# Attention and mixture of experts on one core: stores without order among themselves, gates fetched together, deeper buffers

## The chip, the core and the metric

One core of a Trainium2 chip. Its engines run in parallel, each through its own queue in order: TensorE (PE, with its weight loads, PEld), VectorE (DVE), ScalarE (ACT), GpSimd (POOL) and SyncE (SP, which here only issues DMAs). Indirect DMAs (gathers and scatters by a list of indices) are issued on POOL; the weights come through SP's queue. All transfers run on 16 DMA engines. The metric is the device time of one execution in microseconds, median of several runs.

## The reference

Attention over 8 batches, 12 heads, 448 positions and a head size of 64, with capped scores, and behind it a mixture of experts with 3584 tokens of width 768, 8 experts of width 1024, and room for 80 tokens an expert.

```python
scores = cap * np.tanh(scale * np.matmul(q, k.transpose(0, 1, 3, 2)) / cap)
attn = np.exp(scores - max); attn = attn / (sum(attn) + 1e-09)
x = np.matmul(attn, v)                       # to (B * S, H * D)
logits = x @ w_gate; expert_idx = argmax(logits); gate_w = softmax(logits)[expert_idx]
for e in range(E):
    tok_idx = tokens of e, at most `capacity` of them by gate_w
    out[tok_idx] = gate_w[tok_idx, None] * (np.maximum(x[tok_idx] @ w1[e], 0) @ w2[e])
```

Rows of tokens that no expert keeps are zero.

## The kernel before

Attention runs in 24 units (a batch and four heads), software-pipelined, with an order written out by hand; the work between (gates of a batch, ranks of its tokens, lists of kept tokens) is put into gaps by a planner with costs and due times (`background`, with the queues `urgent`, `low` and `bg`). Attention's rows go to DRAM (`xs`), the gate of each token to DRAM (`gd`). The expert stage is built for at most six experts that hold tokens (`NV`): the first four (`NPRE`, experts 0 to 3 below) are known after five of the eight batches, their rows are fetched during attention's end (`first_rows`: three indirect gathers an expert, 128 descriptors each, and DVE transposes). The last two (experts 4 and 5 below) are known only when all tokens are ranked.

An expert is two runs of jobs: "a" is x times w1 in 6 chunks of 512 KB, "b" is h times w2 in 8 chunks of 384 KB; a chunk is 24 matmul records in the trace (L842). The jobs' order on TensorE is a0 a1 b0 a2 b1 a3 b2 b3 a4 a5 b4 b5. Weights come chunk by chunk through SP into a ring of WPRE + WMORE = 8 + 6 buffers; a chunk's DMA waits until the chunk 14 before it is used up.

Behind "b" stands `put`: it scales the rows by the gate (L890 on DVE; for the last expert L885 on ACT and L887 on DVE, in three parts) into the tile ys, of which there is one buffer, and issues three indirect stores on POOL (L892). The framework orders two stores to `out` as it would any two writes to one tensor: the later one waits on POOL until the earlier one has landed. The gates of expert v are fetched on POOL by three indirect DMAs (`gates`, L777) that are issued when "b" of v begins, so behind the stores of the expert before.

Among expert 2's and 3's products the planner lays the last steps of the ranking: flags `gb` on DVE (L491) and tiny matmuls `pd` (L507) that count them; the rank (L1285, L1289); the marks `rh`, half on DVE and half on POOL (L730) with `rt` on POOL (L735); the matmuls `pcp` that place the tokens (L745, L748); the indices (`listed`, L751 to L763); the fetch of the rows of experts 4 and 5 (L784, three buffers xg); their transposes (L1504). TensorE stands at pcp until both halves of `rh` are there, and its queue is in order. On POOL the order is: stores of expert 2, gates of expert 3, `rh`, `rt`, row fetches of experts 4 and 5, stores of expert 3, gates of expert 4, and so on.

Of the kernel before, what the change touches and what calls it, by code (L numbers as in the profile page):

```python
# [16 lines left out]
B, H, S, D = 8, 12, 448, 64  # L17
# [27 lines left out]
KD = DM // 128  # L45
KF = F // 128
WPRE = 8
WMORE = 6
DIRECT = (20, 23)
NG = SL // 32  # L50
QF = F // 4
# [63 lines left out]
def attn_moe(ctx, tc, q2, k, v, cap, wg, w1, w2, capacity, ct, out):  # L115
# [65 lines left out]
    sg0 = consts.tile([128, NPRE, NG], I32, name="sg0")  # L181
# [389 lines left out]
    def prune(krow, sm, pl):  # L571
# [83 lines left out]
            gather_rows(z["ga"], tks, gi0, OB * S)  # L655

        def rows_out():
            scatter_rows(gp_tile, tks, z["ga"], si0, sg0)

        def gp_tile(key):  # L660
            return tile_([32, NPRE, NG], F32, key)
# [9 lines left out]
        def first_rows():  # L671
            for v in range(NPRE):
                for i in range(3):
                    yield 300, lambda v=v, i=i: fetch(v, i), int(v == i == 0)
                for i in range(3):
                    yield 400, lambda v=v, i=i: lay(v, i), 3 * int(i == 0)
        yield 300, heads, 0
        yield 200, use(0, counts), 1
        steps = order(sm)
# [75 lines left out]
    def scatter_rows(tile_of, tk, a, si, sg):  # L755

        o = tile_of("to")
        nc.vector.tensor_scalar(o, tk, 0.0, BIG, op0=ALU.is_equal, op1=ALU.mult)
        nc.vector.tensor_tensor(o, o, tk, op=ALU.add)
        for i in range(4):  # L760
            w = slice(32 * i, 32 * i + 32)
            nc.vector.tensor_scalar(si[w], o, float(i - 4), None, op0=ALU.add)
            nc.vector.tensor_scalar(sg[w], a, 0.25, -1.0, op0=ALU.mult, op1=ALU.add)  # L763

    def indices(sm, tk, n):
# [4 lines left out]
        scatter_rows(lambda key: sm.tile([32, n, NG], F32, name=key, tag=key), tk, a, si, sg)  # L770
        return gi, si, sg

    def gates(fp, sg, tag, n=T):
# [6 lines left out]

    def fetched(fp, gi, tag, n=T, to=None):

        xg = to if to is not None else fp.tile([128, NP * 32], F32, name=f"xg{tag}", tag="xg", bufs=3)
        nc.gpsimd.indirect_dma_start(out=xg, out_offset=None, in_=xs[0:n].rearrange("t i p c -> (t i) (p c)"),  # L784
                                     in_offset=bass.IndirectOffsetOnAxis(ap=gi, axis=0))
        return xg
# [90 lines left out]
        product(yp, h, ws[KD:], DM)  # L877
        put(fp, yp, gt, si, tag)

    def put(fp, yp, gt, si, tag, last=False):  # L880
        ys = fp.tile([128, NG, QD], F32, name=f"ys{tag}", tag="ys", bufs=1)
        if last:
            for g in range(NG):
                if g % 2 == 0:
                    nc.scalar.activation(ys[:, g], spot(yp, g, QD), AF.Copy, scale=gt[:, g:g + 1])  # L885
                else:
                    nc.vector.tensor_scalar(ys[:, g], spot(yp, g, QD), gt[:, g:g + 1], None, op0=ALU.mult)  # L887
        else:
            y = yp.rearrange("p a (b c) -> p (a b) c", c=QF)[:, 0:NG, 0:QD]
            nc.vector.tensor_tensor(ys, y, gt.rearrange("p (g a) -> p g a", a=1).broadcast_to([128, NG, QD]), op=ALU.mult)  # L890
        for g in range(NG):
            nc.gpsimd.indirect_dma_start(out=out.rearrange("t (i c) -> (t i) c", c=QD), out_offset=bass.IndirectOffsetOnAxis(ap=si[:, g:g + 1], axis=0),  # L892
                                         in_=ys[:, g], in_offset=None, bounds_check=4 * T - 1, oob_is_err=False)

    def compare(sm, tk):

# [594 lines left out]

    def listed():
        tk = fin["tk"] = fin["pcp"][0:32, 0:3 * NV].rearrange("p (e k) -> p e k", k=3)
        fin["gi"], fin["si"], fin["sg"] = indices(fr, tk, NV)
# [24 lines left out]
    st["vector"] = vector  # L1519
    hp, hs, ht, yp, gt = {}, {0: hs0}, {}, {}, {}  # L1520
    more(WPRE + WMORE)
    for i, (k_, vi, kk) in list(enumerate(jobs))[KD:]:
        more(i + WPRE + WMORE)
        if i + 3 == len(jobs):
            while bg or low:
                background(1e9)
            decide(fin["m"], compare(fr, fin["early"]))
        if k_ == "a" and kk == 0:
            st["there"](vi)
        if k_ == "a":  # L1530
            if kk == 0:
                if vi < NV - 1:
                    hp[vi] = pfh.tile([128, 2, 512], F32, name=f"hp{vi}", tag="hp")
                else:
                    hp[vi] = tuple(misc(f"hp{vi}{i_}") for i_ in "ab")
            chunk(hp[vi], xv[vi] if vi >= NPRE else xt0[vi], wts[i], kk, KD - 1, F)
            if kk == KD - 1:
                hs[vi] = relu(fp, hp[vi], f"v{vi}", 1 + (vi == NV - 1))
        else:
            if kk == 0:  # L1540
                yp[vi] = (pft.tile([128, 2, 512], F32, name=f"yp{vi}", tag="ht") if vi < NV - 1 else
                          (pft.tile([128, 512], F32, name=f"yp{vi}a", tag="ht"), pfh.tile([128, 512], F32, name=f"yp{vi}b", tag="hp")))
                gt[vi] = gates(fp, sg0[:, vi], f"v{vi}", OB * S) if vi < NPRE else gates(fp, fin["sg"][:, vi], f"v{vi}")
            chunk(yp[vi], ht[vi], wts[i], kk, KF - 1, DM)
            if kk == KF - 1:
                put(fp, yp[vi], gt[vi], (si0 if vi < NPRE else fin["si"])[:, vi], f"v{vi}", vi == NV - 1)
# [57 lines left out]
```

## Time and profile before

| | us |
|---|---|
| median of 3 runs | 521.21 (519.57 to 523.6) |
| the profiled execution | 522.82 |
| its span, first to last instruction | 521.0 |

| engine | busy us | share of the span |
|---|---|---|
| PE | 467.9 | 90% |
| PEld | 252.3 | 48% |
| DVE | 247.9 | 48% |
| ACT | 324.6 | 62% |
| POOL | 244.4 | 47% |

The mean granted TensorE clock is 0.958 of full speed. A row of the timelines reads: start, duration, engine, line, operation, output and input tiles, count, and in brackets the engine's idle time just before and what ended it. The time of an indirect DMA on POOL is that of its issue; it lands later. Where a wait was for several things, the view names the one that came last by its own reckoning.

### The profile page before, as it was taken

The page shows a single profiled execution, that of the slowest core. Times are in us where ns is not written, and L with a number is a line of the kernel's source. Part 1 is how long each engine was busy: PE and PEld are TensorE (multiplying, and loading weights), DVE is VectorE, ACT ScalarE, POOL GpSimd, SP SyncE. Part 2 cuts the span into 40 slices and gives each one's busy share as a digit, 9 for nine tenths or more (in the row PEclk, how much of TensorE's full clock was granted, in tenths as well). Part 3 has the DMA queues.
Part 4 walks back from the last instruction along what each step waited for, and adds up shares of the span by engine and source line. Part 5 has one row for each costly group of instructions (what it writes and reads, how often), then busy time and mean ns, then how long its engine had stood idle before and what let it go on. Part 6 is the DMA issues. An engine that isn't in the chain of part 4 may idle for free. (4 is left out here: it accounts for less than half of the span.)

```text
span 521.0 us, 21478 instructions
## 1 busy us (share of the span) xinstructions
PE 467.9 (90%) x9591; PEld 252.3 (48%) x9591; DVE 247.9 (48%) x761; ACT 324.6 (62%) x311; POOL 244.4 (47%) x160
## 2 busy tenths in 40 slices
PE   7899999999999999999999999999999976189930
PEld 3344444544444545444554455354576654146820
DVE  1033643564365555667785837655378360040000
ACT  5999899899899989989998979730111100001100
POOL 1766566665655666556566046623101422453051
PEclk9999999999999999999999999999799989589985
DMA  6866786585685696474456738485679979267400
GB/s 165 232 180 179 196 245 180 161 229 171 188 255 153 181 260 180 119 216 127 120 156 165 213 103 253 140 299 172 195 263 352 383 235 348 111 185 256 157 29 16
DMA packets 68647, 101.12 MB, mean 194 GB/s; under 512 B 12833, under 2 KB 50993, under 8 KB 68545
## 3 DMA queue, kind: packets, MB, share of 16 engines
q1 hardware_dynamic: 66048, 96.23, 61.6%
q0 software_dynamic: 2304, 3.26, 2.2%
q8 instruction: 77, 1.26, 1.0%
q14 instruction: 26, 0.20, 0.1%
q10 hardware_dynamic: 192, 0.17, 0.1%
HBM read 76.12 MB, written 23.80 MB: 192 GB/s over the span
## 5 line engine op out<-in xcount | busy, mean ns | idle before, releaser
L1152 ACT ACTIVATE e<-sc,scl 128x896 f32<-128x896 f32 x168 | 163.7, 1006 | 27.5 <-PE sc L1151 19.9
L1156 ACT ACTIVATE e<-e,capt 128x1792 f32<-128x1792 f32 x96 | 153.4, 1598 | 0.0
L1162 POOL TENSOR_TENSOR t<-e 128x896 f32<-128x896 f32 x44 | 92.8, 2110 | 101.7 <-ACT e L1156 100.6
L1151 PE MATMUL sc<-qt,kt 64*32 64x448 f32 x2304 | 132.7, 547 | 4.4 <-ACT e L1152 3.9
L1171 PE MATMUL av<-e,vr 128*32 128x224 f32 x2304 | 129.1, 355 | 1.0 <-DMA vr<-in_v_dram 0.5
L1164 POOL TENSOR_TENSOR t<-t,e 128x896 f32<-128x896 f32 x44 | 92.7, 2107 | 39.5 <-PE sc L1151 19.1
L1171 PEld LDWEIGHTS av<-e,vr 128*32 128x32 f32 x2304 | 67.8, 109 | 61.1 <-issue 18.0
L1211 DVE STREAM_TRANSPOSE st<-sp 128x448 f32<-128x448 f32 x24 | 15.6, 650 | 119.7 <-PE sp L1201 115.8
L892 POOL DMA_INDIRECT out_dram<-ysv,si x18 | 21.0, 1168 | 92.3 <-DMA out_dram<-ysv,si 41.2
L1151 PEld LDWEIGHTS sc<-qt,kt 64*32 64x32 f32 x2304 | 33.0, 106 | 57.6 <-issue 42.7
L842 PE MATMUL hp<-w,xt 128*32 128x256 f32 x720 | 48.6, 393 | 4.2 <-issue 2.6
L842 PE MATMUL yp<-w,thv 128*32 128x192 f32 x960 | 48.0, 350 | 1.3 <-issue 1.3
L1203 PE MATMUL av<-e,vr 64*32 64x224 f32 x384 | 42.9, 350 | 0.2 <-issue 0.2
L1203 PE MATMUL av<-e,vx 64*32 64x224 f32 x384 | 41.3, 350 | 0.0
L842 PEld LDWEIGHTS yp<-w,thv 128*32 128x32 f32 x960 | 34.4, 117 | 12.1 <-issue 4.4
L842 PEld LDWEIGHTS hp<-w,xt 128*32 128x32 f32 x720 | 25.7, 112 | 23.2 <-issue 10.6
L1203 PEld LDWEIGHTS av<-e,vr 64*32 64x32 f32 x384 | 20.1, 106 | 22.5 <-issue 13.1
L418 DVE TENSOR_SCALAR_CACHE_REDUCE gb<-krow,kc 112x896 bf16<-112x896 f32 (+7 forms) x36 | 30.1, 884 | 0.0
L1201 PE MATMUL sp<-e,ones 64*32 64x224 f32 x384 | 28.7, 350 | 0.4 <-issue 0.4
L1224 DVE TENSOR_TENSOR x<-av,r 128x448 f32<-128x448 f32 x48 | 27.8, 620 | 2.4
L1233 DVE STREAM_TRANSPOSE xb<-x 128x448 f32<-128x448 f32 x48 | 28.1, 624 | 0.8
L858 ACT ACTIVATE hsv<-hp 128x768 f32<-128x768 f32 x5 | 4.1, 811 | 33.5 <-PE hp L842 25.5
(241 smaller groups left out, 444.0 us busy)
## 6 DMA issues: line engine op xcount, KB each, us to landing
w<-in_w_dram SPq DMA_DIRECT2D x36, 512.0 KB
w<-in_w_dram SPq DMA_DIRECT2D x48, 384.0 KB
vr<-in_v_dram SPq DMA_DIRECT2D x24, 512.0 KB
out_dram<-zero SPq DMA_DIRECT2D x14, 768.0 KB
xs<-xb SPq DMA_DIRECT2D x32, 336.0 KB
kt<-in_k_dram SPq DMA_DIRECT2D x46, 224.0 KB
qt<-in_q_dram SPq DMA_DIRECT2D x46, 224.0 KB
vx<-in_v_dram SPq DMA_DIRECT2D x48, 32.0 KB
```

Source lines behind the costliest of these rows:

```text
L418: nc.vector.tensor_scalar(g, krow[:, x:y], kp, 0.0, op0=ALU.is_ge, op1=ALU.add, accum_out=a)
L842: nc.tensor.matmul(spot(ps, g, q)[32 * j:32 * j + 32], of(g), w[:, q * j:q * j + q], start=(kk == 0 and g % 2 == 0), stop=(kk == last and ...
L1151: nc.tensor.matmul(ps[32 * m:32 * m + 32, h, :S], st["k", u][w, pr, y:y + 32], st["q", u][w, pr], start=True, stop=True)
L1152: nc.scalar.activation(st["e", u][:, 2 * x:2 * x + 2], ps[:, :, :S], AF.Tanh, scale=scl)
L1156: nc.scalar.activation(e, e, AF.Exp, scale=capt)
L1162: nc.gpsimd.tensor_tensor(t1, e[:, 0:2], e[:, 2:4], op=ALU.add)
L1164: nc.gpsimd.tensor_tensor(st["es", u, pr], st["es", u, pr], e[:, 4:6], op=ALU.add)
L1171: nc.tensor.matmul(st["av", u, i][32 * g:32 * g + 32, HQ * f:HQ * f + HQ], st["v", u][:, g // 2, g % 2, c, 32 * f:32 * f + 32], chunk_of(u ...
L1201: nc.tensor.matmul(st["sp", u][32 * g:32 * g + 32, HQ * i:HQ * i + HQ], st["ones"][w, 0:32], e, start=(part == 0), stop=(part == 1))
L1203: nc.tensor.matmul(st["av", u, i][32 * g:32 * g + 32, HQ * f:HQ * f + HQ], last_of(u, pr, h, i)[w, 32 * f:32 * f + 32], e, start=False, st ...
L1224: nc.vector.tensor_tensor(st["x", u][:, :, w], st["av", u, i][:, :S].rearrange("p (f s) -> p f s", f=2), st["r", u][:, w].rearrange("p (a ...
L1233: nc.vector.transpose(st["xt", b][:, :, j, :], st["x", u][:, f].rearrange("p (a b) -> p a b", b=32))
```

## The change

- The stores of result rows are declared independent of one another (`others`): a store then waits for its scaled rows, and for no other store.
- The gates of experts 0 to 3 are fetched by three indirect DMAs with 128 indices each (32 an expert) into one tile gq, as the last items of `first_rows`; those of experts 4 and 5 in the same manner into gq2, behind their row fetches. When "b" of an expert begins, four ACT copies lay its gates out over the 128 partitions (`gates_of`). The index steps change with that (`gate_rows`).
- Two buffers for ys (from one), six for fetched rows xg (from three), ten more weight buffers behind the first eight (from six).

```diff
-WMORE = 6
+WMORE = 10
...
+            for i in range(NG):
+                yield 100, lambda i=i: gates_at(gq, sg0, i, NPRE, OB * S), 0
...
+    def gate_rows(a, sg, n):
+        for e in range(n):
+            nc.vector.tensor_scalar(sg[32 * e:32 * e + 32], a[:, e], 0.25, -1.0, op0=ALU.mult, op1=ALU.add)
+
+    def gates_at(to, sg, g, n, m):
+        nc.gpsimd.indirect_dma_start(out=to[0:32 * n, g:g + 1], out_offset=None, in_=gd[0:m],
+                                     in_offset=bass.IndirectOffsetOnAxis(ap=sg[0:32 * n, g:g + 1], axis=0))
+
+    def gates_of(fp, packed, e, tag):
+
+        gt = fp.tile([128, NG], F32, name=f"gt{tag}", tag="gt")
+        for i in range(4):
+            nc.scalar.copy(gt[32 * i:32 * i + 32], packed[32 * e:32 * e + 32])
+        return gt
...
-        xg = to if to is not None else fp.tile([128, NP * 32], F32, name=f"xg{tag}", tag="xg", bufs=3)
+        xg = to if to is not None else fp.tile([128, NP * 32], F32, name=f"xg{tag}", tag="xg", bufs=2 * NG)
...
-        ys = fp.tile([128, NG, QD], F32, name=f"ys{tag}", tag="ys", bufs=1)
+    def put(fp, yp, gt, si, tag, last=False, others=None):
+        ys = fp.tile([128, NG, QD], F32, name=f"ys{tag}", tag="ys", bufs=2)
...
+            if others is not None:
+                for o in others:
+                    tc.declare_no_dep(w.ins, o.ins, reason="rows of different tokens")
+                others.append(w)
...
+        for i in range(NG):
+            low.append((100, lambda i=i: gates_at(gq2, fin["sg"][:, 0], i, NV - NPRE, T), 0))
...
-                gt[vi] = gates(fp, sg0[:, vi], f"v{vi}", OB * S) if vi < NPRE else gates(fp, fin["sg"][:, vi], f"v{vi}")
+                gt[vi] = gates_of(fp, gq, vi, f"v{vi}") if vi < NPRE else gates_of(fp, gq2, vi - NPRE, f"v{vi}")
```

## Rows read from the trace of the kernel before

**Rows 1.** The page: GB/s in 40 slices of 13.0 us; the chain's last piece.

```profile
GB/s 165 232 180 179 196 245 180 161 229 171 188 255 153 181 260 180 119 216 127 120 156 165 213 103 253 140 299 172 195 263 352 383 235 348 111 185 256 157 29 16
...
510.96 0.69 POOL out_dram L892
```

**Rows 2.** Waits from 380 us: who waited for whom, us in total, times, longest.

```profile
POOL out_dram L892 <- DMA out_dram<-ysv,si: 41.2, 11, 5.8
...
PE pcp L745 <- POOL rh L730: 13.7, 1, 13.7
```

**Rows 3.** Timeline of POOL from 395 us: gates, stores, marks, row fetches.

```profile
408.74 0.94 POOL L777 DMA_INDIRECT gtv<-gd,sg  x1 [0.30 <-issue]
415.32 2.48 POOL L892 DMA_INDIRECT out_dram<-ysv,si  x1 [5.64 <-DVE ysv L890]
...
428.37 1.15 POOL L892 DMA_INDIRECT out_dram<-ysv,si  x1 [4.66 <-DMA out_dram<-ysv,si]
...
432.39 0.94 POOL L777 DMA_INDIRECT gtv<-gd,sg  x1 [0.31 <-issue]
439.79 1.02 POOL L892 DMA_INDIRECT out_dram<-ysv,si  x1 [6.45 <-DVE ysv L890]
...
453.39 0.69 POOL L730 TENSOR_TENSOR rh<-oh,bo 112x288 bf16<-112x288 bf16 x1
...
456.23 0.98 POOL L784 DMA_INDIRECT xgv<-xs,gi  x1 [1.93 <-DVE to L758]
...
464.86 0.94 POOL L784 DMA_INDIRECT xgv<-xs,gi  x1 [0.30 <-issue]
```

**Rows 4.** Timeline of DVE from 380 us: scalings, indices, the last transpose.

```profile
414.29 0.76 DVE L890 TENSOR_TENSOR ysv<-yp,gtv 128x576 f32<-128x576 f32 x1 [8.37 <-DMA gtv<-gd,sg]
...
438.75 0.76 DVE L890 TENSOR_TENSOR ysv<-yp,gtv 128x576 f32<-128x576 f32 x1 [9.75 <-PE yp L842]
...
455.25 0.71 DVE L753 TENSOR_SCALAR gi<-ga 32x18 int32<-32x18 f32 x4
...
468.43 0.38 DVE L1504 STREAM_TRANSPOSE xt<-xgv 128x192 f32<-128x192 f32 x1 [1.04 <-DMA xgv<-xs,gi]
```

**Rows 5.** Timeline of ACT: the first scaling of the last expert.

```profile
503.02 0.42 ACT L885 ACTIVATE ysv<-yp5a,gtv 128x192 f32<-128x192 f32 x1 [15.89 <-DMA gtv<-gd,sg]
```

**Rows 6.** Timeline of PE from 395 us: products, and the waits between them.

```profile
397.60 8.01 PE L842 MATMUL yp<-w,thv 128*32 128x192 f32 x192
...
420.70 0.38 PE L507 MATMUL pd<-ones_b,gb 112*128 112x1 bf16 x9 [2.59 <-DVE gb L491]
...
427.06 3.13 PE L842 MATMUL yp<-w,thv 128*32 128x192 f32 x71
...
454.13 0.47 PE L745 MATMUL pcp<-rh,lh 112*32 112x24 bf16 x12 [13.74 <-POOL rh L730]
...
462.15 4.28 PE L842 MATMUL hp<-w,xt 128*32 128x256 f32 x60 [1.14 <-DVE xt L1504]
...
492.05 0.83 PE L842 MATMUL yp5a<-w,thv 128*32 128x192 f32 x16
...
499.52 0.51 PE L842 MATMUL yp5b<-w,thv 128*32 128x192 f32 x8
```

**Rows 7.** Windows: us, engines' busy us (instructions), granted clock, DMA share, GB/s.

```profile
360.00:370.00 10.00, 7.64 (x75) 3.26 (x71) 7.65 (x31) 0.81 (x1) 5.36 (x7) 0.75 0.52 145
...
390.00:418.00 28.00, 27.91 (x524) 19.16 (x516) 17.65 (x58) 3.58 (x5) 10.14 (x8) 1.00 0.99 367
...
430.00:434.00 4.00, 2.80 (x26) 0.78 (x19) 0.00 (x0) 0.00 (x0) 2.73 (x3) 1.00 0.99 270
...
440.00:454.00 14.00, 0.39 (x12) 0.32 (x13) 0.00 (x0) 0.00 (x0) 6.30 (x7) 0.62 0.47 187
454.00:461.00 7.00, 6.87 (x100) 4.37 (x99) 3.46 (x23) 0.16 (x1) 3.17 (x5) 0.53 0.39 118
...
478.00:482.00 4.00, 3.08 (x43) 1.43 (x35) 0.00 (x0) 0.00 (x0) 2.00 (x3) 1.00 0.48 140
```

More of the change, by code (lines that the diff above doesn't have):

```diff
@@ L180, in attn_moe @@
     si0 = consts.tile([128, NPRE, NG], I32, name="si0")
-    sg0 = consts.tile([128, NPRE, NG], I32, name="sg0")
+    sg0 = consts.tile([32 * NPRE, NG], I32, name="sg0")
+    gq = consts.tile([32 * NPRE, NG], F32, name="gq")
+    gq2 = consts.tile([32 * (NV - NPRE), NG], F32, name="gq2")
     xt0 = [consts.tile([128, KD, SL], F32, name=f"xt0_{v}") for v in range(NPRE)]
@@ L657, in rows_out @@
         def rows_out():
-            scatter_rows(gp_tile, tks, z["ga"], si0, sg0)
+            scatter_rows(gp_tile, tks, z["ga"], si0)
+            gate_rows(z["ga"], sg0, NPRE)
         def gp_tile(key):
@@ L753, in gather_rows, with scatter_rows @@
             nc.vector.tensor_scalar(gi[32 * i:32 * i + 32], a, float(i - 4), None, op0=ALU.add)
-    def scatter_rows(tile_of, tk, a, si, sg):
+    def gate_rows(a, sg, n):
[9 more added lines that the diff above has]
+        return gt
+    def scatter_rows(tile_of, tk, a, si, sg=None):
         o = tile_of("to")
@@ L762, in scatter_rows, with indices @@
             nc.vector.tensor_scalar(si[w], o, float(i - 4), None, op0=ALU.add)
-            nc.vector.tensor_scalar(sg[w], a, 0.25, -1.0, op0=ALU.mult, op1=ALU.add)
-    def indices(sm, tk, n):
+            if sg is not None:
+                nc.vector.tensor_scalar(sg[w], a, 0.25, -1.0, op0=ALU.mult, op1=ALU.add)
+    def indices(sm, tk, n, packed=None):
         a = sm.tile([32, n, NG], F32, name="ga", tag="ga")
@@ L769, in indices @@
         gather_rows(a, tk, gi, T)
-        scatter_rows(lambda key: sm.tile([32, n, NG], F32, name=key, tag=key), tk, a, si, sg)
+        scatter_rows(lambda key: sm.tile([32, n, NG], F32, name=key, tag=key), tk, a, si, sg if packed is None else None)
+        if packed is not None:
+            gate_rows(a[:, packed], sg[:, 0], packed.stop - packed.start)
         return gi, si, sg
@@ L878, in ffn2 @@
         put(fp, yp, gt, si, tag)
-    def put(fp, yp, gt, si, tag, last=False):
-        ys = fp.tile([128, NG, QD], F32, name=f"ys{tag}", tag="ys", bufs=1)
+    def put(fp, yp, gt, si, tag, last=False, others=None):
+        ys = fp.tile([128, NG, QD], F32, name=f"ys{tag}", tag="ys", bufs=2)
         if last:
@@ L891, in put @@
         for g in range(NG):
-            nc.gpsimd.indirect_dma_start(out=out.rearrange("t (i c) -> (t i) c", c=QD), out_offset=bass.IndirectOffsetOnAxis(ap=si[:, g:g + 1], axis=0),
-                                         in_=ys[:, g], in_offset=None, bounds_check=4 * T - 1, oob_is_err=False)
+            w = nc.gpsimd.indirect_dma_start(out=out.rearrange("t (i c) -> (t i) c", c=QD), out_offset=bass.IndirectOffsetOnAxis(ap=si[:, g:g + 1], axis=0),
+                                             in_=ys[:, g], in_offset=None, bounds_check=4 * T - 1, oob_is_err=False)
+            if others is not None:
+                for o in others:
+                    tc.declare_no_dep(w.ins, o.ins, reason="rows of different tokens")
+                others.append(w)
     def compare(sm, tk):
@@ L1493, in listed @@
         tk = fin["tk"] = fin["pcp"][0:32, 0:3 * NV].rearrange("p (e k) -> p e k", k=3)
-        fin["gi"], fin["si"], fin["sg"] = indices(fr, tk, NV)
+        fin["gi"], fin["si"], fin["sg"] = indices(fr, tk, NV, slice(NPRE, NV))
         fin["early"] = fr.tile([32, NPRE, 3], F32, name="early", tag="early")
@@ L1519, in attn_moe @@
     st["vector"] = vector
+    stored = []
     hp, hs, ht, yp, gt = {}, {0: hs0}, {}, {}, {}
@@ L1542, in attn_moe @@
                           (pft.tile([128, 512], F32, name=f"yp{vi}a", tag="ht"), pfh.tile([128, 512], F32, name=f"yp{vi}b", tag="hp")))
-                gt[vi] = gates(fp, sg0[:, vi], f"v{vi}", OB * S) if vi < NPRE else gates(fp, fin["sg"][:, vi], f"v{vi}")
+                gt[vi] = gates_of(fp, gq, vi, f"v{vi}") if vi < NPRE else gates_of(fp, gq2, vi - NPRE, f"v{vi}")
             chunk(yp[vi], ht[vi], wts[i], kk, KF - 1, DM)
             if kk == KF - 1:
-                put(fp, yp[vi], gt[vi], (si0 if vi < NPRE else fin["si"])[:, vi], f"v{vi}", vi == NV - 1)
+                put(fp, yp[vi], gt[vi], (si0 if vi < NPRE else fin["si"])[:, vi], f"v{vi}", vi == NV - 1, stored)
                 if vi < NV - 1:
```

## The prediction

> **What bounds the kernel now.** I read the page first (the slices, for where the engines thin out), then the chain that ended last, the waits after 380 us, the timelines of POOL, DVE and PE there, and last the windows. Up to about 380 us TensorE is busy throughout, and the change touches little there. What counts is the expert stage behind it: TensorE needs 1.0 us for a w2 chunk (192 matmul records, 8 chunks, in 8.01 us [rows 6]), and the weights are ahead of it, for in the longest stall the DMA engines fall to 0.47 of their time with nothing left to fill [rows 7]. So TensorE's own stalls set the end, and behind most of them stands POOL's queue, which runs in order. The reader is to see three things in it.
>
> First, each store of an expert's rows waits until the store before it has landed: 41.2 us in 11 waits [rows 2]. Secondly, the three gate fetches of the next expert are queued behind these stores: those of expert 1 end at 409.7 us, and DVE's scaling of expert 1's rows (L890) starts only at 414.29, 8.37 us after DVE was free and about as long after TensorE had finished that product (405.6) [rows 3, 4, 6]. For expert 2 the product was finished at 430.2, the gates were issued until 433.3, the scaling came at 438.75; the view names TensorE there, but it had long been done, so it was again the gates' DMA [rows 3, 4, 6]. Thirdly, behind expert 2's stores and expert 3's gates stands the little product `rh` (0.69 us), which starts at 453.39, while TensorE waits 13.7 us for it before it can place the tokens of the last two experts [rows 2, 3, 6]. From `rh` hangs everything behind: pcp, indices (gi done at 455.96), the fetch of expert 4's rows, its first matmul at 462.15, and from there 37.9 us to TensorE's last matmul at 500.0 [rows 3, 4, 6]. Then comes a tail of 21.0 us to the end of the span at 521.0: expert 5's gates were fetched behind expert 4's stores, so the first scaling starts 3.0 us after TensorE is done [rows 5, 6], three stores follow in single file, the last one issued until 511.65, and 9.35 us go by after it [rows 1].
>
> **The change part by part.** *Gates for four experts at once.* 18 fetches of about 0.95 us become 3 ahead of the experts and 3 for the last two. The first three follow the early row fetches in attention's end (their indices are made in `rows_out`, ahead of these), so experts 0 to 3 never wait for gates. Added: 4 ACT copies of 32 by 3 elements an expert; no row shows this form, and the bounds are nothing and the 0.42 us of the far larger ACT scaling [rows 5], under 1.7 us an expert. ACT is busy 3.6 of the 28 us from 390 and idle 15.9 us ahead of its last scaling [rows 5, 7], which covers them: nothing; uncovered they would delay the copy of h that TensorE needs for "b", by their own length. The last two experts' gates would matter only if they landed after expert 5's relu, some 15 us after they are issued.
>
> *Middle, from 405 us.* Scaling of expert 1 at 405.9 and not 414.29: DVE's chain moves up by 8.4 us, so the flags (gb) for which TensorE waits from 418.1 to 420.7 are there at 412.3 [rows 4, 6]. TensorE goes on from 418.1: two groups of tiny matmuls (0.6 us each) and the six remaining chunks of expert 2's product, 7.2 us, finished at 425.3 instead of 430.2. Scaling to 426.2 (0.76 us), stores from 426.4. Unordered, each takes its issue of 1.0 us and a gap of 0.3, the pace of the fetches [rows 3]; the three end at 430.0, no gates follow, `rh` at 430.3 instead of 453.39. With the steps as they are now (`rh` and `rt` 1.0, pcp 0.9, indices 0.9, gap 0.3), the first row fetch of expert 4 starts at 433.4 instead of 456.23, and the third ends at 436.9.
>
> When do these rows land? Between 2.6 us after the issue (465.80 to the transpose at 468.43) and 4.6 us (the gates, 409.68 to 414.29, DMA engines 0.99 busy) [rows 3, 4, 7]. TensorE now runs without the long stall before it, so the weights' DMA will be full: I take 4.6. Rows at 441.5, transposes 0.4, expert 4 starts at 441.9 instead of 462.15: **20.2 us** gained. By then TensorE has used up its work at about 435 and waits some 7 us: the row fetch is what is late next. From there I keep the 37.9 us of before. They hold two slow stretches beside triples of fetches; those go in part, but a stall of 7 us brings some microseconds at the lower clock level, as the seven after the long stall (0.53 granted, near the 1.2 GHz level) [rows 7]. TensorE ends at 479.8.
>
> *Tail.* Gates present, ys in another buffer: scaling 0.1 us after TensorE, 0.42 long, 0.28 to the store's start (as from 439.51 to 439.79) [rows 3, 4, 5], three issues with two gaps 3.7 us, then the 9.35: 13.8 us instead of 21.0, **7.2 us** gained.
>
> A rule of the Trainium skill bears on the stores' price: DMA: Bandwidth & Descriptors, section Anatomy of one DMA, gives a software DMA a fixed 2.0 us and its bytes at 436 GB/s, an estimate of 2.2 us for a store of 98 KB. Of the 41.2 us the rows show 3.7 a wait, so the trace charges more than the rule while the weights stream; by the rule alone the eleven waits would be worth some 24 us.
>
> *More buffers.* Six for fetched rows: in the last stage the second expert's fetches no longer wait for the first one's transposes; they are wanted 8 us later than the first's, so nothing. In the early stage POOL issues the row fetches of experts 1 to 3 sooner, about 10 us. That matters because TensorE runs badly beside three or more fetches in a row: 26 matmuls in 4 us at 430 to 434 and 43 at 478 to 482, where 390 to 418 has 19 a microsecond, and 75 in the 10 us from 360, with six fetches behind one another [rows 3, 7]. The same 15 indirect DMAs now fall into the end of attention. Between losing 4 us there and gaining the 7 us that the stretch at 360 loses, I take a gain of **1.5 us**. Ten weight buffers more than the eight, instead of six: the page's last full slices sum to 26.4 MB from 391 to 495 us [rows 1], 72 us at the 367 GB/s of rows 7, so they could all be in by 463, some 15 us before TensorE needs the last; weights weren't late and won't be. The four buffers overlay memory of the last attention unit, so one chunk is issued a few microseconds later, 20 us before its use: nothing. Two buffers for ys keep the scaling from waiting for stores; counted above.
>
> **Sum**: profiled run 522.8 (span 521.0 and 1.8 around it) - 20.2 - 7.2 - 1.5 = **494 us** (493.9). The profiled run lies 1.6 us above the median of 521.2, inside the runs' spread, so I take nothing off for it.
>
> **Rivals.**
> *Stores in a row slow TensorE as fetches do.* For: every stretch with three fetches in a row has the dip. Against: three single stores during expert 5's product cost nothing (its 8 chunks take 8.0 us from 492.05 to 500.0, the pace of 397.60) [rows 6]; but those were 3 us apart. A triple costs 1.7 to 2.6 us by the windows (43 and 26 matmuls of some 75). Expert 2's is covered by the new 7 us wait; those of experts 0, 1, 3 and 4 cost 7 to 10: 501 to 504 us.
> The Trainium skill (Runtime: NRT & Kernel Launch, section Instruction fetch mechanics) says that an engine's instructions are streamed in by its own DMA queue and that this is mostly hidden. By that this rival would cost nothing; the dips of rows 7 happen all the same, and no row says what causes them.
>
> *The order stays* (the declaration doesn't remove the waits). Gates and buffers still work. Expert 2's stores then end near 438.5 (two waits of 5), `rh` 439, expert 4 at 451, TensorE 489; the tail saves only 3.5: 507 us.
>
> *The weights become the bound.* Against: the 15 us above. A mean of 280 GB/s instead of 367 would do it: 94 us, the last chunk in at 485, TensorE done at 486 and not 480: 500 us.
>
> *Not faster: TensorE's clock doesn't come back.* It falls in the new 7 us wait, and the dips beside nine fetches and three stores in a row keep it at the lower level. Before, it rose 7 us after a 14 us stall. All 33 us of the remaining work at half speed would add 33: about 524 us; from some 30 us at half speed on there is no gain, and with expert 3's product too it is 532, slower.
>
> *The early stretch gains fully* (7 instead of 1.5) and rows land in 2.6 us: 486.
>
> **How the numbers follow.** Forecast 0.6, with its own range 487 to 500; stores slowing TensorE 0.2; order stays 0.05; weights 0.04; early gain 0.07; clock 0.04. The range must leave out no more than 0.2: 484 to 507 holds all but the clock case and edges of the others. What a measurement of this kernel can tell from no change is about 1%, 5 us: all cases but the clock's lie beyond it. Faster 0.95, same 0.02, slower 0.03.
>
> **What would show it.** Right: stores of one expert 1.3 us apart on POOL; the waits for out_dram gone; L890 within 0.3 us of its product's end for every expert; `rh` on POOL directly behind expert 2's third store, near 430; TensorE's longest wait then for the transposes of expert 4's rows, 4 to 8 us; the first scaling of expert 5 directly behind the last matmul, and 14 us from there to the end. Wrong: dips of TensorE beside stores (first rival); stores 3 to 6 us apart (order stays); waits of TensorE for w (weights); a granted clock near 0.5 for longer than 8 us behind the wait.

## The result, and the profile after

The changed kernel takes 508.0 us (median of four runs, 506.6 to 509.2) where the kernel before takes 521.8: a ratio of 0.974, 95% interval 0.969 to 0.979. The forecast was 494.0, with a range of 484 to 507. The sign and most of the mechanism were right; the gain is half of the forecast.

One thing has to be said first, because the numbers can't be read without it: the experiments met several chips. On one of them, met twice, the kernel before takes 522 or 523 us, as it did here; on five others it takes 509 to 511. Each ratio below is to the kernel before on the same chip; "here" and "the 521 us chip" mean one that behaves as in the profile shown before, "the 509 us chips" the others.

The order is gone, as the timeline of POOL shows (start, duration, line, tiles, and in brackets idle time and what ended it). To be set beside [rows 3]:

```profile
432.58 0.98 POOL L915 DMA_INDIRECT out_dram<-ysv,si  x1 [14.10 <-DVE ysv L913]
433.87 0.98 POOL L915 DMA_INDIRECT out_dram<-ysv,si  x1 [0.30 <-issue]
435.16 0.98 POOL L915 DMA_INDIRECT out_dram<-ysv,si  x1 [0.30 <-issue]
436.15 0.69 POOL L735 TENSOR_TENSOR rh<-oh,bo 112x288 bf16<-112x288 bf16 x1
...
442.42 1.00 POOL L807 DMA_INDIRECT xgv<-xs,gi  x1 [5.36 <-DVE fm L943]
...
448.75 0.94 POOL L807 DMA_INDIRECT xgv<-xs,gi  x1 [0.30 <-issue]
449.99 0.90 POOL L765 DMA_INDIRECT gq<-gd,sg  x1 [0.30 <-issue]
...
456.25 0.98 POOL L915 DMA_INDIRECT out_dram<-ysv,si  x1 [0.30 <-issue]
...
495.50 0.98 POOL L915 DMA_INDIRECT out_dram<-ysv,si  x1 [5.79 <-ACT ysv L908]
...
498.08 0.98 POOL L915 DMA_INDIRECT out_dram<-ysv,si  x1 [0.30 <-issue]
```

The stores of an expert are 1.3 us apart, `rh` stands directly behind expert 2's third store (436.15 instead of 453.39), and no store waits for another (41.2 us in [rows 2]). But from 442.42 to 457.2 twelve indirect DMAs now follow one another 0.3 us apart: six row fetches, three gate fetches, expert 3's three stores.

TensorE's timeline gives the milestones: the first matmul of expert 0's second product ("b0" below), the first of expert 4, and the last of all.

```profile
385.21 4.11 PE L865 MATMUL yp<-w,thv 128*32 128x192 f32 x96
...
449.67 1.08 PE L865 MATMUL hp<-w,xt 128*32 128x256 f32 x8 [6.09 <-DVE xt L1531]
...
494.43 0.61 PE L865 MATMUL yp5b<-w,thv 128*32 128x192 f32 x5
```

Before, b0 started at 379.31, expert 4 at 462.15, and the last matmul ended at 500.03 [rows 6]. So the span's 14.1 us less (506.9 instead of 521.0) are made of four terms:

| stretch | before | after | change | forecast |
|---|---|---|---|---|
| to b0's start | 379.3 | 385.2 | +5.9 | -1.5 |
| b0's start to expert 4's | 82.8 | 64.5 | -18.4 | -20.2 |
| expert 4's start to the last matmul | 37.9 | 45.4 | +7.5 | 0 |
| tail | 21.0 | 11.9 | -9.1 | -7.2 |

The two large gains are there. Two stretches that were to gain a little or nothing lost 13.4 us. The waits of PE from 325 us on name what stands in them:

```profile
PE hp L865 <- DVE xt L1531: 6.1, 1, 6.1
PE av L1230 <- issue: 5.7, 9, 0.9
PE hp L865 <- issue: 3.4, 5, 1.2
```

The first is the new wait for expert 4's rows that the prediction named. "Issue" is time in which the engine waited for nothing that the profile shows. The windows (columns as in [rows 7]) show where; in brackets is the number of instructions:

```profile
332.00:336.00 4.00, 2.64 (x40) 0.77 (x18) 2.44 (x13) 0.44 (x1) 3.06 (x4) 1.00 0.27 76
336.00:340.00 4.00, 2.06 (x6) 0.62 (x7) 0.00 (x0) 0.00 (x0) 2.62 (x3) 0.74 0.70 209
340.00:344.00 4.00, 3.81 (x35) 1.51 (x33) 0.00 (x0) 3.18 (x3) 0.00 (x0) 0.50 0.41 158
...
448.00:452.00 4.00, 2.15 (x20) 0.54 (x24) 1.14 (x3) 0.00 (x0) 3.09 (x4) 0.50 1.03 393
452.00:456.00 4.00, 2.80 (x29) 1.19 (x26) 1.14 (x3) 0.00 (x0) 3.03 (x4) 0.75 1.04 384
456.00:460.00 4.00, 2.05 (x10) 0.66 (x13) 0.00 (x0) 0.00 (x0) 0.98 (x1) 0.67 0.51 190
```

Six matmuls in 4 us at 336 to 340, ten at 456 to 460, and the granted clock is at 0.50 (the level of 1.2 GHz) behind each: in 340 to 344, and in 460 to 464, which is not shown. Both stops lie beside long rows of indirect DMAs on POOL: seven row fetches from 330.77 to 339.24 us, where the three buffers of before made rows of three, and the twelve just shown. A third stop lies at 353 to 359, beside three row fetches and three gate fetches (350.91 to 358.4).

### The profile page after: what moved, and what is told of

It is laid out like the page before. It is cut to its first block, busy times and chain, and to the rows that moved or that the text cites. A ratio compares the mean times of both kernels' runs of the same rounds, so it can differ in the third digit from the quotient of the medians.

```text
span 506.9 us, 21472 instructions
## 1 busy us (share of the span) xinstructions
PE 470.9 (93%) x9591; PEld 254.8 (50%) x9591; DVE 248.5 (49%) x759; ACT 329.0 (65%) x335; POOL 231.8 (46%) x148
## 3 DMA queue, kind: packets, MB, share of 16 engines
q8 instruction: 77, 1.26, 1.0%
## 4 chain that ended last, share of the span: by engine, by line
PE 88%; issue 4%; ACT 2%; DMA 2%; POOL 1%; DVE 1%; SPq 0%; POOLq 0%; DVEq 0%; ACTq 0%
PE sc L1178 24%; PE av L1198 23%; PE hp L865 10%; PE yp L865 8%; PE sp L1208 5%; PE av L1230 5%; PE sc L1170 3%; PE lgp L1277 2%; PE sp L1228 2%; ACT e L1179 1%; DMA w<-in_w_dram 1%; PE pd L426 1%; PE hp5a L865 1%; ACT e L1183 1%; PE htv L893 1%
## 5 line engine op out<-in xcount | busy, mean ns | idle before, releaser
L1198 PEld LDWEIGHTS av<-e,vr 128*32 128x32 f32 x2304 | 68.0, 110 | 60.9 <-issue 18.2
L865 PE MATMUL hp<-w,xt 128*32 128x256 f32 x720 | 50.2, 417 | 9.8 <-DVE xt L1531 6.1
L1230 PE MATMUL av<-e,vx 64*32 64x224 f32 x384 | 43.8, 352 | 3.2 <-issue 3.1
L1230 PE MATMUL av<-e,vr 64*32 64x224 f32 x384 | 44.1, 351 | 2.5 <-issue 2.5
L865 PE MATMUL yp<-w,thv 128*32 128x192 f32 x960 | 43.2, 327 | 1.6 <-issue 1.6
L865 PEld LDWEIGHTS hp<-w,xt 128*32 128x32 f32 x720 | 28.1, 118 | 28.0 <-issue 9.6
L865 PEld LDWEIGHTS yp<-w,thv 128*32 128x32 f32 x960 | 31.5, 110 | 10.7 <-issue 3.7
L1228 PE MATMUL sp<-e,ones 64*32 64x224 f32 x384 | 29.8, 350 | 0.2 <-issue 0.2
```

Of the source, the lines that this page charges most:

```text
L865: nc.tensor.matmul(spot(ps, g, q)[32 * j:32 * j + 32], of(g), w[:, q * j:q * j + q], start=(kk == 0 and g % 2 == 0), stop=(kk == last and ...
L1198: nc.tensor.matmul(st["av", u, i][32 * g:32 * g + 32, HQ * f:HQ * f + HQ], st["v", u][:, g // 2, g % 2, c, 32 * f:32 * f + 32], chunk_of(u ...
L1228: nc.tensor.matmul(st["sp", u][32 * g:32 * g + 32, HQ * i:HQ * i + HQ], st["ones"][w, 0:32], e, start=(part == 0), stop=(part == 1))
L1230: nc.tensor.matmul(st["av", u, i][32 * g:32 * g + 32, HQ * f:HQ * f + HQ], last_of(u, pr, h, i)[w, 32 * f:32 * f + 32], e, start=False, st ...
```

## Experiments

Theories. **A**: a row of indirect DMAs issued back to back on POOL stops TensorE, the longer the row the more; the change made the rows longer. **B**: the four added weight buffers lie over memory of the last attention unit, so SP, which issues in order, stands until 369 us (its waits: 30.4 us for that unit's matmuls, 3.6 before); weights and the last write of attention's rows come late. **C**, formed after the first set: the stops belong to the chip.

SP's waits for that unit's matmuls from 325 us on, after and before (us in total, times, longest):

```profile
SPq L842 <- PE av L1198: 30.4, 2, 20.0
```

```profile
SPq L819 <- PE av L1171: 3.6, 1, 3.6
```

### First set: parts undone (509 us chip)

```diff
 e1:  xg ... bufs=2 * NG  ->  bufs=3
 e2:  WMORE = 10  ->  WMORE = 6
 e3:  both
 e4:  put(..., stored)  ->  put(...)        # stores ordered again
```

> The changed kernel with the buffers for fetched rows back at three instead of six; everything else of the change stays. Theory A (indirect DMAs issued in a row on GpSimd starve TensorE, and the longer the row the more): the rows of 7 and of 6 early fetches break into threes again, the first b0 matmul comes back from 385.2 to 379 to 381 us, the span of 333 to 341 us no longer stands still, and the row of 12 after expert 4's start becomes 3 + 9 with a wait between, worth another 0 to 2 us: 500 to 504 us in all against 508.0. Theory B (the deeper weight queue is to blame): the early stretch stays at 385 and the time at 507 to 509 us.

> The changed kernel with six instead of ten late weight buffers. Theory A (rows of indirect DMAs): no change, 506 to 510 us, the first b0 matmul still at 385 us and 45 us from expert 4's first to the last matmul. Theory B (the deeper weight queue blocks SyncE until 369 us, delays the last write of activation rows and with it the row fetches of expert 4, which began at 442.4 us although their indices were there at 440.3): expert 4's first matmul some 2 us earlier and 45 us back towards 38: 498 to 503 us.

> Both undone: three buffers for fetched rows and six late weight buffers; what is left of the change is the freed order of stores, the second buffer of scaled rows and the gates fetched for several experts at once. Theory A: like the kernel with three row buffers alone, 500 to 504 us. Theory B: like the one with six weight buffers alone, 498 to 503 us, and the one with three row buffers alone at 508. If both have a part, it is faster than either, 494 to 499 us.

> The changed kernel with the stores of result rows ordered among themselves as before; all else of the change stays. My reading of the middle stretch (each store of a row waits some 4 us for the one before it): the stores of experts 0 to 2 again 4 us apart, the marks of the last batch behind expert 2's stores 6 to 9 us later, and so expert 4's first matmul; the tail back from 11.9 to 21 us; but fewer indirect DMAs back to back behind expert 4's start, so that 45.4 us from there to the last matmul shrink by 2 to 4: 518 to 524 us. If the order did not matter (rival): 506 to 510 us.

Measured, beside 509.1 of before: e1 485.8 (ratio 0.953), e2 477.6 (0.941), e3 479.6 (0.942), e4 497.5 (0.979). All missed their expectations in absolute time, since these were set against 508 and 522. Between kernels of the set: six weight buffers instead of ten are worth 6.2 us (e1 to e3), so B has a part. And e2 and e4 have the same seven early fetches in a row, yet TensorE had no issue wait beside them: A does not hold on this chip.

### Second set: the same kernels beside one another (521 us chip)

```diff
 a2:  the changed kernel       b2:  the kernel before       e7:  as e2
 e6 (on the kernel before):  WMORE = 6  ->  WMORE = 10
```

> The changed kernel once more, unaltered, beside the kernel before, because the first four experiments ran where the kernel before took 509.1 us instead of 521.8. Theory A (a row of indirect DMAs on GpSimd starves TensorE in every execution of this program): TensorE again nearly stops at 333 to 341 us, 353 to 359 us and 454 to 459 us with waits that no semaphore explains. Theory C (those stops belong to the chip or the execution: the kernel with the stores ordered again had the same seven fetches in a row from 331.6 to 340.0 us and no stop): no stop, or stops elsewhere, and the first b0 matmul near 367 to 373 us. The ratio to before again 0.965 to 0.98 by either.

> The kernel before, unaltered, for a trace from the same chip as the others of this set. Where the kernel before takes 509 us and not 522, theory C says that the 13 us lie in its own stops beside gate and row fetches (336.5 to 339, 346 to 348.5, 361.5 to 368, 430 to 434, 478 to 482 us in the first trace), which are then mostly gone; if they are all there, the 13 us lie elsewhere.

> The kernel before with one part of the change alone: ten late weight buffers instead of six. Theory B (the four added buffers lie where the last attention unit's exponentials lie, so that SyncE, which issues in order, stands until that unit is done, and the weights, the last write of activation rows and what follows come late): SyncE's waits for the last unit's matmuls 12 to 20 us in a piece, DMA idle there, first b0 matmul 3 to 6 us later; in all 4 to 10 us slower than before. Prediction's reading (more weight buffers bring nothing and cost nothing): within 1.5 us of before.

> The changed kernel with six late weight buffers once more, now beside the unaltered changed kernel on the same chip. Theory B: 8 to 20 us faster than the changed kernel, ratio to before 0.935 to 0.95 again. If the four buffers matter little and the first set merely met a faster chip: within 3 us of the changed kernel.

Measured, beside 523.1: a2 508.2 (0.974), b2 521.2, e6 524.6 (1.005, interval 1.002 to 1.009), e7 507.1 (0.971). The stops of the changed kernel are back at the same places (issue waits 12.6 us in all from 325 us on), those of the kernel before too (b2: 7.5 us), and e7, the program that took 477.6 us in the set before, has them too. So C holds: the same program stops on one chip and not on another. e6 is at the edge of the prediction's reading (within 1.5 us) and below B's 4 to 10: SP stood and DMA fell idle as B said (a share of 0.01 from 350 to 355 us, 0.92 in the kernel before), but the late write was issued by 429.75, and the row fetch that reads it came only at 456.93, behind `rh`. e7's 1.1 us less than a2 are within the runs' spread, so B's 8 to 20 us did not come: e7 gained 2.7 us at the row fetch (55.2 us behind b0's start instead of 57.9), but then DVE stood 10.3 us ahead of expert 3's scaling, with expert 4's transposes queued behind. The view gives no cause. The times of the semaphores' updates, which lie in the trace and which no view prints, do: TensorE's signal that this product is done came at 454.82, 0.08 us before the scaling, though the view lets its last matmul start at 444.68. So DVE waited for TensorE; what held the signal back no run shows.

### Third and fourth set: rows spaced, doses, and the change alone (509 us chips)

```diff
 e8, e11:
+    def space():                       # idle: a 128x512 scratch tile
+        nc.gpsimd.memset(idle, 0.0); nc.gpsimd.memset(idle, 0.0)
...  space() ahead of each indirect DMA but the stores of experts 2 and 5
 e5, e12 (on the kernel before), at units 5, 7, 9, ... 19 of attention:
+    1 fetch; 2; 3; 6; 3 of 4 bytes; 3 stores; 3 with one fill between; 3 with two
 e9: as e1     e10: as e4     a3: the changed kernel
```

> The changed kernel with two fills of a scratch tile (128x512) on GpSimd ahead of each indirect DMA of the early fetches and gates, of the last experts' row and gate fetches, and of the stores but those of experts 2 and 5: by the 0.41 us of a 112x352 fill in the trace some 1.2 us more between two of them, a period near 2.4 us instead of 1.26. Where the kernel before takes some 521 us (as in the first trace and in the last set): theory A (in a row of indirect DMAs TensorE's next instructions aren't fetched; packets of that queue show none from 329.2 to 341.4 us there, two in the same stretch where before takes 509 us): instruction packets land between the spaced DMAs, no stop at 333 to 341, 353 to 359 and 454 to 459 us, the first b0 matmul back from 385 to 372 to 379 us, 494 to 500 us in all. If the number of indirect DMAs counts and not their spacing: 506 to 512 us. Where before takes 509 us: no stops to remove, 0 to 3 us slower than the changed kernel would be there.

> The changed kernel with three instead of six buffers for fetched rows, as in the first set, there 485.8 beside 509.1 of before. Where before takes 521 us, theory A: the row of seven breaks into threes, the stop of 333 to 341 us shrinks to the 2 or 3 us of the kernel before, and the first b0 matmul comes at 378 to 382 instead of 385 us; the row of twelve becomes 3 + 9: 501 to 506 us. If the row's length doesn't count: 506 to 510 us. Where before takes 509 us: 485 to 487 us again.

> The changed kernel with the stores ordered among themselves again, in the first set 497.5 beside 509.1 of before. Where before takes 521 us: expert 4's first matmul 7 to 12 us later than the 449.7 of the changed kernel (its marks stand behind nine stores that wait 4 to 7 us each), the tail 20 us instead of 12, less lost behind expert 4's start as the row of twelve is shorter: 516 to 524 us. If the freed order brings nothing: 506 to 510 us. Where before takes 509 us: 496 to 500 us again.

> The kernel before with indirect DMAs added in the attention stage that nothing reads but themselves (fetches of 768 B a row, of 4 B a row, and stores of 768 B a row to a scratch tensor), one dose to every second unit: in order 1 fetch, 2 in a row, 3, 6, 3 of 4 bytes, 3 stores, 3 fetches with a fill of 256 columns between two, 3 with two fills of 512 between. Where before takes 521 us, theory A: no stop beside 1, 0 to 1 us beside 2, 1 to 3 us beside each 3 whatever they move, 5 to 8 us beside 6, at most 1 us beside the 3 with a short fill and none beside the 3 with two long fills; instruction packets of TensorE's queue missing beside each stop. If it is what the rows move and not their issue: nothing beside the 4-byte ones. If the stops need the loaded DMA of the experts' stage: none at all. Where before takes 509 us: none at all.

> The changed kernel, unaltered. Where before takes 521 us: 508 us again, with stops at 333 to 341, 353 to 359 and 454 to 459 us. Where before takes 509 us: by theory A without those stops, so without the 5.9 and 7.5 us that they cost: ratio 0.945 to 0.965, 481 to 491 us. If the stops are not what costs them, the ratio is 0.974 there too, 496 us.

> The changed kernel with fills of a scratch tile between the indirect DMAs, as before: a period of 2.5 us instead of 1.26. Where before takes 521 us, theory A (the row's density keeps TensorE's instructions from being fetched): no stop at 333 to 341 and at 353 to 359 us, first b0 matmul at 372 to 379 us, 494 to 500 us. If their number counts and not their spacing: 506 to 512 us. Where before takes 509 us: 487 us again.

> The kernel before with doses of indirect DMAs in the attention stage (in order 1 fetch, 2 in a row, 3, 6, 3 of 4 bytes, 3 stores, 3 with one short fill between, 3 with two long fills between). Where before takes 521 us, theory A: stops of TensorE without a semaphore, none beside 1, up to 1 us beside 2, 1 to 3 us beside each plain row of 3 whatever it moves, 5 to 8 us beside 6, less beside the filled rows. If the stops need the loaded DMA of the experts' stage: none. Where before takes 509 us: none, as in the first look.

Measured, beside 509.7 and 509.6: e8 487.4 (0.955), e9 483.6 (0.948), e10 498.8 (0.977), e5 512.8; a3 481.6 (0.945, interval 0.939 to 0.951), e11 489.0 (0.959), e12 514.0. The doses made no stop here. The changed kernel alone gains 28 us where no row stops TensorE, as theory A said (481 to 491); its only issue waits from 325 us on are 0.4 and 2.0 us, at the end of expert 3's product. Its first early fetches stand as here, seven in a row, and these are its windows, to be set beside those of the section above:

```profile
332.00:336.00 4.00, 4.00 (x120) 2.19 (x104) 2.81 (x13) 3.89 (x4) 3.08 (x4) 1.00 0.30 80
336.00:340.00 4.00, 3.65 (x83) 2.17 (x76) 3.76 (x10) 3.78 (x4) 2.50 (x3) 1.00 0.77 222
...
436.00:440.00 4.00, 4.00 (x76) 2.24 (x72) 0.65 (x2) 0.00 (x0) 3.01 (x3) 0.93 1.04 385
```

And its milestones:

```profile
366.42 4.11 PE L865 MATMUL yp<-w,thv 128*32 128x192 f32 x96
...
431.70 1.94 PE L865 MATMUL hp<-w,xt 128*32 128x256 f32 x16 [8.50 <-DVE xt L1531]
...
467.01 0.51 PE L865 MATMUL yp5b<-w,thv 128*32 128x192 f32 x8
```

The order of the stores is worth 16 to 17 us there (e4 and e10 against a3): expert 4 starts 74.8 us after b0 with it and 65.3 without, and the tail is 18.9 to 19.4 us instead of 11.9. In e4 POOL waits as before the change,

```profile
POOL out_dram L915 <- DMA out_dram<-ysv,si: 48.2, 11, 6.4
```

and TensorE waits 15.4 us for `rh`. That is 4.4 us a wait. The Trainium skill (DMA: Bandwidth & Descriptors, section Anatomy of one DMA) would make it 2.2 by the estimate quoted in the prediction; the measurement decides, and under the weights' stream it is twice as much.

Six weight buffers: in the changed kernel (a3) and with six (e2), on POOL,

```profile
415.95 0.69 POOL L735 TENSOR_TENSOR rh<-oh,bo 112x288 bf16<-112x288 bf16 x1
...
424.91 1.00 POOL L807 DMA_INDIRECT xgv<-xs,gi  x1 [8.05 <-DMA w<-in_w_dram]
```

```profile
415.64 0.70 POOL L735 TENSOR_TENSOR rh<-oh,bo 112x288 bf16<-112x288 bf16 x1
...
418.46 1.01 POOL L807 DMA_INDIRECT xgv<-xs,gi  x1 [1.90 <-DVE to L778]
```

With ten buffers the row fetch starts 9.0 us after `rh`, with six 2.8. The view names a weight transfer; what the fetch reads is the last write of attention's rows, which SP issues behind the weights, until 415.5 in a3 and until 410.6 in e2:

```profile
409.49 6.00 SPq L1264 DMA_DIRECT2D xs<-xb  x4
```

```profile
405.86 4.69 SPq L1264 DMA_DIRECT2D xs<-xb  x4
```

When it lands no view says, but the semaphores' updates do: its last part lands at 423.81 in a3 and at 415.87 in e2. In the ten runs of the changed kernel with ten weight buffers and free stores, spaced ones included, the fetch starts 1.1 us after this landing, 2.1 to 8.7 us after its indices; in the ten others it starts 0.3 us after its indices. So it is this write that is late.

### Last set: rows and doses on the chip that stops

Spaced rows and doses went into one kernel, so that one execution on a 521 us chip would answer both. It met 509 us chips twice (e13, e14) and the 521 us chip once (e15).

```diff
 e13, e14, e15:  e8 with the doses of e5; idle in bf16, also for the doses' fills
```

> The changed kernel with fills of a scratch tile (two of 512 columns) between its indirect DMAs, and in its attention stage the doses that only touch scratch data: 1 fetch, 2 in a row, 3, 6, 3 of 4 bytes, 3 stores, 3 with one fill of 256 columns between, 3 with two of 512 between. Where before takes 521 us, theory A: stops without a semaphore beside the plain rows of 3 (1 to 3 us each, the 4-byte ones too) and of 6 (5 to 8 us), none beside 1 and beside the rows with two long fills; in the experts' stage no stops at 333 to 341 and 353 to 359 us of the kind of the changed kernel, and 496 to 504 us with the doses' own cost. If number and not spacing counts: stops beside the filled rows as beside the plain ones, and 508 to 516 us. If stops need the loaded DMA of the experts' stage: none in attention. Where before takes 509 us: no stops, 487 to 493 us.

> The kernel of the run before once more: the changed kernel with fills between its indirect DMAs, and the doses in attention (1 fetch, 2 in a row, 3, 6, 3 of 4 bytes, 3 stores, 3 with a short fill between, 3 with two long fills between). Where before takes 521 us, theory A: stops without a semaphore beside the plain rows of 3 (1 to 3 us each) and of 6 (5 to 8 us), none beside 1 and beside the rows with two long fills; none of the stops of 333 to 341 and 353 to 359 us; 496 to 504 us. If number and not spacing counts: stops beside the filled rows too, 508 to 516 us. Where before takes 509 us: 491 us again.

> The changed kernel with fills between its indirect DMAs and the doses in attention, a last time. Where before takes 521 us, theory A: stops without a semaphore beside the plain rows of 3 (1 to 3 us each) and of 6 (5 to 8 us), none beside 1 and beside the rows with two long fills; no stops at 333 to 341 and 353 to 359 us; 496 to 504 us. If number and not spacing counts: stops beside the filled rows too, 508 to 516 us. Where before takes 509 us: 490 us again.

Measured: e13 490.9 (beside 510.8), e14 489.4 (beside 509.9), e15 506.4 (beside 521.9). The doses touch only scratch data, so what they cost shows in the time from one dose to the next, e15 against e14 (first the row of six, then the three of 4 bytes; the other doses alike):

```profile
162.76 0.96 POOL L1459 DMA_INDIRECT dgt<-xs,dgi  x1
...
169.05 0.95 POOL L1459 DMA_INDIRECT dgt<-xs,dgi  x1 [0.30 <-issue]
198.46 0.97 POOL L1463 DMA_INDIRECT dg<-gd,dgi  x1
```

```profile
158.88 0.96 POOL L1459 DMA_INDIRECT dgt<-xs,dgi  x1
...
165.15 0.95 POOL L1459 DMA_INDIRECT dgt<-xs,dgi  x1 [0.30 <-issue]
186.30 0.96 POOL L1463 DMA_INDIRECT dg<-gd,dgi  x1
```

From the row of six to the next dose pass 35.7 us on the chip that stops and 27.4 on the other: the row costs 8.3 us. TensorE's windows of 10 us from the row's start, e15 and then e14:

```profile
162.80:172.80 10.00, 7.63 (x88) 2.48 (x80) 0.08 (x2) 5.00 (x4) 7.79 (x8) 0.90 0.54 163
```

```profile
158.90:168.90 10.00, 10.00 (x238) 4.97 (x232) 3.93 (x11) 9.05 (x8) 8.38 (x8) 1.00 0.70 209
```

| dose (period of its DMAs) | cost on the 521 us chip, us |
|---|---|
| 1 fetch | 0.0 |
| 2 in a row (1.28) | 1.3 |
| 3 in a row (1.26) | 2.0 |
| 6 in a row (1.26) | 8.3 |
| 3 of 4 bytes a row (1.26) | 2.7 |
| 3 stores (1.31) | 3.8 |
| 3 with one fill of 256 columns between (1.47) | 1.9 |
| 3 with two fills of 512 between (2.26) | -0.8 |

Set against e13, the other run on a 509 us chip, the costs are the same within 0.1 us, but for the last, which is 0.1 instead of -0.8.

That is A's pattern: nothing beside one, more with the row's length, whatever the rows move and with no full DMA needed (a share of 0.54 beside the row of six), and gone at a period of 2.3 us. In parts it went otherwise: the short fill helped nothing (1.9 beside 2.0), and six fetches and three stores cost more than the 8 and 3 us at most that were expected. All these DMAs had 128 indices, so whether the DMAs count or their pieces was not tried.

In the experts' stage, where all rows but expert 2's and 5's stores are spaced in this kernel, TensorE's issue waits from the first early fetch on come to 1.4 us, where after and a2 have 11.7 and 12.6, and these are its milestones:

```profile
389.07 4.11 PE L877 MATMUL yp<-w,thv 128*32 128x192 f32 x96
...
453.64 1.08 PE L877 MATMUL hp<-w,xt 128*32 128x256 f32 x8 [8.81 <-DVE xt L1574]
...
491.12 0.59 PE L877 MATMUL yp5b<-w,thv 128*32 128x192 f32 x8
```

The stretches come out nearly as on the 509 us chips:

| kernel, chip | first early fetch to b0 | b0 to expert 4 | expert 4 to last matmul | tail |
|---|---|---|---|---|
| before, 521 | 55.2 | 82.8 | 37.9 | 21.0 |
| after, 521 | 61.3 | 64.5 | 45.4 | 11.9 |
| after, spaced and dosed (e15), 521 | 43.8 | 64.6 | 38.1 | 14.4 |
| before, dosed (e5), 509 | 43.8 | 83.5 | 35.8 | 23.1 |
| after (a3), 509 | 42.6 | 65.3 | 35.8 | 11.9 |
| after, six weight buffers (e2), 509 | 42.6 | 59.3 | 36.6 | 12.3 |

The tails of dosed kernels hold 2 to 3 us of the doses: from the last store's issue to the end pass 11.0 us in e5, and 9.4 and 9.0 in the two traces of the kernel before; 10.2 to 10.8 in e13 to e15, and 7.3 and 7.9 in e8 and e11. The doses also made e15's first early fetch 19.9 us later than e14's (345.31 and 325.44). They cost more than A's 496 to 504 us allowed for, and 506.4 lies between that and its rival's 508 to 516, so the time alone decides nothing here; the stretches do. Without the doses the spaced kernel would take some 484 us on this chip (506.4 - 19.9 - 2.5, an estimate; it was not run there alone), against 508 for the changed one. On the 509 us chips the fills only cost, and more than the 0 to 3 us expected: 487 to 489 against 482.

## Why the prediction was right and wrong

*Middle, -20.2.* Right: -18.4 here, -18.2 on the 509 us chips (e5 to a3). The chain was as told: scalings without a wait for gates, `rh` behind the third store, the row fetch late next, a wait of 6 us. The 1.8 us short are a balance: counted from b0, the indices came 1.3 us later than forecast, and the row fetch 1.8 us later still, 2.1 us after its indices (442.42; gi done at 440.3) and not 0.3; 1.3 were made good, as TensorE began on the first third of the rows and not on all three. The four ACT copies, put at nothing, took 0.8 us an expert.

*More weight buffers: "nothing".* Wrong where there are no stops. The text named the overlay and looked at the delayed chunk's own use, but not at SP's queue behind it: SP stood 12 to 20 us in a piece, then the weights ran with DMA full, and the last write of attention's rows came late. In the kernel before, 13.7 us of waiting for `rh` hid that (e6: +1.5 us). The change took away this cover with its other hand: ten buffers cost 6.2 us on the 509 us chip (e1 to e3, both with three row buffers; with six, b0 to expert 4 takes 65.3 us in a3 and 59.3 in e2).

*"From there I keep the 37.9 us."* The step that failed here: 45.4. The prediction had the six row fetches and three gates on POOL and let the slow stretches beside them go "in part", but it did not lay expert 3's stores behind them: twelve in a row. On the 509 us chips, where rows don't stop TensorE, the step holds to the tenth (35.8 and 35.8).

*Early stretch, -1.5.* The other step that failed: +5.9 here. The bounds were a loss of 4 and a gain of 7, and I took a small gain; a triple cost 1.7 to 2.6 us in the trace before, and I let all fifteen indirect DMAs cost no more than 4, without asking how long a row the six buffers would make. A row of six stood in the trace before, three row and three gate fetches from 358.57 to 366.03, and the text itself took it for 7 us, the stretch at 360; the change moved it to 350.91 and made one of seven ahead of it. The doses show that the cost grows faster than the number: 2.0 us for three, 8.3 for six. The weight buffers have no part in it: from the first early fetch to b0 pass 55.2 us in the kernel before with ten of them (e6), as without, and 62.7 in the changed kernel with six (e7). That three row buffers alone would have kept it from this loss is not shown, as e1 and e9 met only 509 us chips. On those the term is -1.2 (43.8 to 42.6).

*Tail, -7.2.* Right in kind, larger in size: -9.1 here. (The -11.2 from e5 to a3 hold some 2 us of e5's doses.) After the last issue 7.8 us go by, not 9.35.

The first scaling of expert 5 starts where TensorE ends, as forecast:

```profile
494.81 0.42 ACT L908 ACTIVATE ysv<-yp5a,gtv 128x192 f32<-128x192 f32 x1 [14.23 <-issue]
```

*The sum.* -28.9 was forecast; on the 509 us chips the change is worth -28.0 (481.6 from 509.6), though there in part by luck, by errors that cancel: with six weight buffers the middle would have gained 4 us more than forecast (83.5 to 59.3 in e2) and the tail gained 2 more, and the ten buffers lost 6. Here it is -13.8.

*The rivals.* The first, stores in a row slow TensorE as fetches do, was right in kind and was given 0.2. It priced only triples of stores (7 to 10 us, 501 to 504 us), and of these expert 0's cost nothing and expert 4's some 2 us: in 6 us around them TensorE has 98 matmuls here and 98 in a3, and 100 here and 156 in a3. The price lay in fetches, gates and stores that stand in one row once nothing parts them. The rule that the prediction set beside it, from the Trainium skill (Runtime: NRT & Kernel Launch, section Instruction fetch mechanics), has instructions streamed in and the streaming mostly hidden; by it missing instructions would not be what stops TensorE. Order stays, weights as TensorE's bound and a clock that doesn't come back are refuted: no wait between stores, no wait of TensorE for w, and the clock at 0.50 in four stretches of 6.8 us before TensorE's end, each time back at 1.00.

## What to carry to other kernels

A wait that a change removes may have been the only thing that kept indirect DMAs apart on GpSimd's queue, or the cover of a transfer that was late anyway: write down the queue's new order over all parts of the change, rows and all, and ask of each hidden delay what hides it now. Price a long row by a row of that length, not by a short one times a factor. And before a small gain is believed, see whether the same program stops on another chip: here the same edit was worth 14 us on one and 28 on others, and the version with six weight buffers is nowhere behind the changed kernel, with ratio 0.941 on a 509 us chip and 0.971 on the 521 us chip (its lead over the changed kernel is within the spread on the latter, and on the former was measured only from one chip to another, 477.6 and 481.6 us).

## What was unexpected of the hardware

Chips differ in this and in little else that these runs show: the changed kernel reaches its first early fetch at 323.93 us here and at 323.78 in a3, and the 12 us between the kernel before on the two kinds of chip are about the 11.4 us that its early stretch loses to stops (55.2 and 43.8). What differs between the chips no run shows.

Nor is it settled how a row stops TensorE. One reading is that its next instructions aren't fetched. The queues' packets from 329.5 to 341 us, here,

```profile
q0 software_dynamic: 252, 0.54, 19.3%
q14 instruction: 3, 0.02, 0.6%
```

and in a3, where TensorE went on,

```profile
q0 software_dynamic: 254, 0.53, 16.4%
q8 instruction: 2, 0.03, 1.1%
q14 instruction: 2, 0.02, 0.3%
```

show that the queue q8 (77 packets in the whole program, on either chip; that it is TensorE's is a guess) brings nothing in while TensorE stands. But an engine that stands asks for nothing, and behind the stop of 353 to 359 us TensorE goes on at 359.54, although no packet of q8 came from 353 to 360. So the missing packets may be the effect and not the cause. Nor need a stop show as idle time of TensorE: its signal that expert 3's product is done comes 0.0 us after the end that the view gives the last matmul in a3, 2.4 us after it here, and 9.8 us after it in e7.
